# Hash-masked attention, capacity routing and two expert layers: late weight splits behind a gather, a fourth conversion buffer, projections in two units

## The chip, the cores and the metric

The kernel runs on one core of a Trainium2 chip. The metric is the device time of one execution in microseconds, taken as the median of several runs. Of the kernel before, three runs stand at 821.13, 822.87 and 824.08 us.

## The reference, cut to what matters

Three stages follow one another, and each needs the one before.

```python
# 1. attention, B=2, H=8, S=768, D=64: a query sees only keys of its own hash bucket
q_bits = (q @ proj > 0); k_bits = (k @ proj > 0)          # 6 bits each
scores = where(q_bucket == k_bucket, q @ k.T / sqrt(D), -1e9)
x = softmax(scores) @ v                                    # -> x of 1536 x 512
# 2. routing: 8 experts of 192 tokens each, then two layers per expert
assigned = greedy_by_logit(x @ w_gate, cap=192)
out[assigned == e] = relu(x[assigned == e] @ w1[e]) @ w2[e]   # 512 -> 1024 -> 512
# 3. a gated layer over all tokens
xn = out / rms(out) * rms_g
return (silu(xn @ w_gate2) * (xn @ w_val)) @ w_out         # 512 -> 1536 -> 512
```

The three weights of stage 3 arrive as 64-bit numbers; the kernel turns each of their blocks into 32-bit numbers itself.

## The kernel before, in words

**Attention.** There are eight pairs of heads (`p`), and each pair has twelve *units* (`u`, 96 in all): one unit is one head and one chunk of 128 queries. The loop at lines 601 to 621 writes, unit by unit, the exponential of the next unit, the transposes of this one (L361), the scores of the one after the next (L336 and L339), the product with the values (L380), and last whatever the table `fill` holds for that unit. So the scores of a pair's first unit are written in the unit that is the eleventh of the pair ahead of it (its unit 10, counting from 0).

`fill` carries three kinds of side work, each put at a unit by hand:

- *Preparing the next pair.* `SLOTS` gives six places, as units after the start of the pair that is running: four for `prep_t` (transposes, then on GpSimd a rounded part `nh` at L285 and a rest `nl` at L286), two for `prep_p` (six matmuls with the hash projections at L294, then a threshold on VectorE at L297). Right after the second `prep_t` of a tensor comes `prep_d`, six DMAs on SyncE's queue (L310 to L312). After the last `prep_p` comes `prep_s`, four DMAs (L320) that bring the hash bits into the second operand of the scores; one unit later `load_pair` issues three loads (L98). The first prepared pair uses `SLOTS1`, which stays as it is.
- *Converting weights of stage 3*, in 36 blocks (lines 528 to 532). Block n is loaded at unit n * 12 // 5 (`conv_load`, L242), converted five units later (`conv`: ScalarE L250, VectorE L253 and L254, then four GpSimd operations L255 to L258 on the tile `ha`), and stored to DRAM four units after that (`conv_store`, L263). The tile `ha` has three buffers.
- *Loading expert weights*: eight loads of 512 KB (`load_w`, L202 and L205), at units 20, 29, 38 and so on.

Within one unit of `fill` the order is: preparation, then conversion, then `load_w`. SyncE issues all of these DMAs in the order written.

**Routing and the experts.** After the last unit ScalarE rounds eight blocks of the first expert's weights (`split_hi`, L215); the rests (`split_lo`, L218: a subtraction on 128 x 1024 numbers) of blocks 0 to 3 are on VectorE (0 to 2 inside the routing rounds, 3 at line 925), and those of blocks 4 to 7 on GpSimd. Each `split_lo` also issues the load of the block eight further on. GpSimd fetches the tokens of the first two experts with three gathers (L890), a conditional block closes the routing, VectorE finishes the output indices (L921 to L923) and block 3's rest, ScalarE loads a table that waits for a small memset (L1053, L1104), and TensorE transposes the gathered rows (`gather_t`: L983; evacuated by ScalarE at L987 and VectorE at L988), between filler matmuls (L1101).

Then the experts run in *steps*, 16 per expert: eight of layer 1 (L1005, L1007) and eight of layer 2 (L1029, L1031). Layer 2's step 8 is the first that reads block 4, steps 10, 12 and 14 the first that read blocks 5, 6 and 7. Work is hung on steps by `at_step`; within one step the order is that of the calls:

```python
at_step(9, gather_t, 0, 2)
for n, i in enumerate(range(4, 8)):
    at_step(LATE[n], split_lo, i, True)      # rests of blocks 4..7 on GpSimd
...
at_step(t0 + WSTEP[n], split_w, 8 * (e + 1) + n, n in DVE_HI, n in POOL_LO)
...
at_step(t0 + 2 + 4 * kk, gather, j + 1, kk)  # steps 2, 6 and 10 of an even expert
```

`gather` has three row buffers, so the next gather waits until TensorE has transposed the first gather's rows. The next expert's first block (its rounding, L213 on VectorE, and its rest on GpSimd) is at step 4, the second at step 7.

**The gated layer** (L1194, L1222) follows with TensorE busy to the end.

Of the kernel before, what the change touches and what calls it, by code (L numbers as in the profile page):

```python
# [13 lines left out]
I32 = mybir.dt.int32  # L14
# [10 lines left out]
ACT_EVAC = 1  # L25
SLOTS1 = (0, 0, 4, 5, 5, 6)
CONV = 5
SLOTS = (-1, 0, 1, 3, 7, 7)
WSTEP = (4, 7, 9, 10, 10, 13, 15, 16)
POOL_LO = (0, 1, 4, 5, 7)  # L30
DVE_HI = (0, 4)
# [5 lines left out]
NORM = (10, 11, 12, 15)  # L37
N5 = (16, 16, 16, 16)
BB = 4
LATE = (0, 0, 1, 3)  # L40
MB = (5, 1, 2)
WB = (8, 0, 2, 0, 4, 4)
MINEXP = float(np.array([0x38100000], np.int32).view(np.float32)[0])
# [3 lines left out]
def lsh_attention__moe__swiglu_kernel(ctx, tc, q, k, v, proj, m_wg, m_w1, m_w2,  # L47
# [38 lines left out]
    cv = att.enter_context(tc.tile_pool(name="cv", bufs=2))  # L86
# [141 lines left out]
    for src, dst in ((f_wg, wg_d), (f_wv, wv_d), (f_wo, wo_d)):  # L228
        n = src.shape[0] * src.shape[1] // (128 * 512)
# [15 lines left out]
    def conv(n):  # L245
        w = CV[n]
        hi = w.bitcast(I32).rearrange("p (n t) -> p n t", t=2)[:, :, 1]
        lo = w.bitcast(U32).rearrange("p (n t) -> p n t", t=2)[:, :, 0]
        lr = cv.tile([128, 512], I32, name="lr")
        nc.scalar.activation(lr, lo, AF.Copy, scale=2.0 ** -29)  # L250
        ha = cv.tile([128, 512], I32, name="ha", bufs=3)
        sg = cv.tile([128, 512], I32, name="sg")
        nc.vector.tensor_scalar(ha, hi, 0x7fffffff, None, op0=OP.bitwise_and)  # L253
        nc.vector.tensor_scalar(sg, hi, -2 ** 31, 2 ** 30, op0=OP.bitwise_and, op1=OP.bitwise_or)  # L254
        nc.gpsimd.tensor_scalar(ha.bitcast(F32), ha.bitcast(F32), 3.0e38, MINEXP, op0=OP.min, op1=OP.max)  # L255
        nc.gpsimd.tensor_tensor(ha, ha, eight.to_broadcast([128, 512]), op=OP.mult)
        nc.gpsimd.tensor_tensor(ha, ha, lr, op=OP.add)
        nc.gpsimd.tensor_tensor(ha, ha, sg, op=OP.add)  # L258
        CV[n] = ha
# [251 lines left out]
    def at(u, f, *a):  # L511
        fill.setdefault(u, []).append((f, a))

    for p in range(1, NPAIR):
        u0 = (p - 1) * TPB * 2
        slots = iter(SLOTS if p > 1 else SLOTS1)
        for nm in "kq":
            for half in range(2):
                n = u0 + next(slots)
                at(n, prep_t, p, nm, half)  # L520
            at(n, prep_d, p, nm)
        for half in range(2):
            n = u0 + next(slots)
# [4 lines left out]
    for n in range(len(convs)):  # L528
        u = CONV + n * 12 // 5
        at(u - 5, conv_load, n)  # L530
        at(u, conv, n)
        at(u + 4, conv_store, n)
    for i in range(8):
        at(20 + i * 9, load_w, i)
    at(HP * TPB * 2 + 7, key_top)
# [456 lines left out]
    def at_step(t, f, *a):  # L992
        todo.setdefault(t, []).append((f, a))
# [118 lines left out]
    for n, i in enumerate(range(4, 8)):  # L1112
        at_step(LATE[n], split_lo, i, True)
    for e in range(E):
# [198 lines left out]
```

## Time and profile before

| what | value |
|---|---|
| median of three runs | 822.87 us (821.13 to 824.08) |
| the profiled execution | 824.88 us |
| span in its profile, first to last instruction | 822.8 us |
| mean granted clock of TensorE | 0.96 of full speed |
| TensorE busy | 768.2 us (93% of the span) |
| VectorE, ScalarE, GpSimd busy | 522.4, 396.1, 329.6 us |
| mean DMA rate | 140 GB/s |

The span is 2.1 us shorter than the profiled execution, which in turn is 2.0 us above the median. In the tables of the trace, "PE" is TensorE, "PEld" its weight loads, "DVE" VectorE, "ACT" ScalarE, "POOL" GpSimd and "SP" SyncE (a "q" behind it: the engine's queue). L12 is line 12 of the kernel. A bracket such as [2.41 <-DMA s_q<-sg] is idle time of that engine just before the instruction and what ended it; "issue" stands where the profile shows nothing that was waited for. A busy engine is not always at work: an instruction that is held by something else is shown as long.

### The profile page before, as it was taken

Reading aid. Unit: us, or ns where it says so; the run is one execution under the profiler, and the core shown is the slowest. Engines: PE = TensorE matmul, PEld = TensorE weight load, DVE = VectorE, ACT = ScalarE, POOL = GpSimd, SP = SyncE. Lnnn points to the kernel's source line nnn. Section 1 sums busy time; section 2 is a strip of 40 time slices with the busy share of each in tenths; the row PEclk is TensorE's granted clock in tenths of the full one; section 3 lists DMA queues with packets and bytes.
Section 4 is the critical chain, followed back from the end, with each engine's and each line's share of the span. In section 5 each row is a group of like instructions: output and inputs, shape, how many; then the busy total and the mean of one; then the engine's idle time right before and its main releaser. Section 6 shows DMA issues by size and latency. Waiting matters only on the chain.

```text
span 822.8 us, 14746 instructions
## 1 busy us (share of the span) xinstructions
PE 768.2 (93%) x5317; PEld 690.7 (84%) x5317; DVE 522.4 (63%) x1342; ACT 396.1 (48%) x863; POOL 329.6 (40%) x309
## 2 busy tenths in 40 slices
PE   7999989999989983489999999999999999999997
PEld 4788878887878863289999999999999999999996
DVE  7788977888768888648878778665422332233222
ACT  3677766676656762056776766653311211121111
POOL 3288876786767720736676652000100010001001
PEclk9999998999989995579999999999999999999999
DMA  3568896987869512247687844264200110001001
GB/s 78 172 205 225 260 252 198 271 255 250 231 205 267 186 39 77 76 170 232 226 269 235 272 148 142 69 223 145 77 1 1 38 39 1 1 1 39 1 0 39
DMA packets 89770, 115.58 MB, mean 140 GB/s; under 512 B 22124, under 2 KB 68188, under 8 KB 89692
## 3 DMA queue, kind: packets, MB, share of 16 engines
q1 hardware_dynamic: 87612, 108.28, 43.8%
q0 software_dynamic: 1920, 6.29, 2.2%
q8 instruction: 44, 0.72, 0.4%
q14 instruction: 34, 0.28, 0.1%
q10 hardware_dynamic: 160, 0.00, 0.0%
HBM read 77.62 MB, written 18.87 MB: 117 GB/s over the span
## 4 chain that ended last, share of the span: by engine, by line
PE 36%; issue 18%; POOL 1%; DVE 1%; ACT 1%; POOLq 0%; ACTq 0%; DVEq 0%
PE pg L1194 6%; PE pv L1194 6%; PE py L1029 6%; PE po L1222 6%; PE ph L1005 5%; PE py L1031 3%; PE ph L1007 3%; POOL out_dram L1230 1%; PE ph L983 1%; DVE wl L218 0%; PE px L1061 0%; POOL wl L218 0%; PE px L1084 0%; ACT bt L1015 0%; ACT sq L1047 0%
## 5 line engine op out<-in xcount | busy, mean ns | idle before, releaser
L1230 POOL DMA_INDIRECT out_dram<-ot,oi x12 | 11.7, 974 | 307.7 <-DVE ot L1228 306.2
L350 ACT ACTIVATE pr<-sc,rs 128x768 f32<-128x768 f32 x96 | 95.3, 993 | 61.9 <-DVE rs L343 35.4
L218 POOL TENSOR_TENSOR wl<-wr,wh 128x1024 fp32r<-128x1024 f32 x39 | 93.9, 2419 | 53.0 <-PE ph L1005 21.7
L341 DVE TENSOR_REDUCE rs<-sc 128x1 f32<-128x768 f32 x96 | 91.2, 950 | 24.6 <-PE sc L339 24.2
L1203 DVE TENSOR_TENSOR a<-sg,pg 128x384 f32<-128x384 f32 x48 | 26.6, 553 | 103.1 <-ACT sg L1201 103.1
L361 PE MATMUL m<-ident,pr 128*128 128x128 f32 x576 | 85.4, 284 | 5.7 <-ACT pr L350 2.6
L1005 PE MATMUL ph<-xg,wh 128*128 128x384 f32 x256 | 76.4, 368 | 8.8 <-issue 6.9
L380 PE MATMUL xo<-pt,ld_v 128*64 128x128 f32 x1128 | 83.9, 285 | 0.0
L361 PEld LDWEIGHTS m<-ident,pr 128*128 128x128 f32 x576 | 63.5, 142 | 20.6 <-issue 6.0
L380 PEld LDWEIGHTS xo<-pt,ld_v 128*64 128x64 f32 x1128 | 60.8, 138 | 19.2 <-issue 12.8
L1029 PE MATMUL py<-ht,wh 128*128 128x384 f32 x256 | 76.4, 363 | 0.0
L1201 ACT ACTIVATE sg<-pg 128x384 f32<-128x384 f32 x48 | 23.5, 490 | 106.0 <-PE pg L1194 105.9
L1207 ACT ACTIVATE ah<-a 128x384 fp32r<-128x384 f32 x48 | 25.2, 525 | 99.6 <-DVE a L1204 99.6
L1194 PE MATMUL pg<-xh,gl 128*128 128x384 f32 x192 | 64.6, 336 | 0.0
L1194 PE MATMUL pg<-xl,gh 128*128 128x384 f32 x192 | 64.6, 336 | 0.0
L1194 PE MATMUL pg<-xh,gh 128*128 128x384 f32 x192 | 64.6, 336 | 0.0
L1194 PE MATMUL pv<-xh,vl 128*128 128x384 f32 x192 | 64.4, 335 | 0.0
L1194 PE MATMUL pv<-xh,vh 128*128 128x384 f32 x192 | 64.4, 335 | 0.0
L1194 PE MATMUL pv<-xl,vh 128*128 128x384 f32 x192 | 64.4, 335 | 0.0
L1031 PE MATMUL py<-ht,wl 128*128 128x192 f32 x256 | 63.5, 253 | 0.0
L363 ACT ACTIVATE pt<-m 128x384 f32<-128x384 f32 x120 | 55.9, 488 | 6.8 <-PE m L361 6.8
L336 PE MATMUL sc<-s_k,s_q 128*128 128x384 f32 x192 | 58.3, 385 | 0.0
(252 smaller groups left out, 1961.3 us busy)
## 6 DMA issues: line engine op xcount, KB each, us to landing
wr<-in_moe_w_dram SPq DMA_DIRECT2D x64, 512.0 KB, 4.8
w<-in_moe_w_gate_dram SPq DMA_DIRECT2D x12, 512.0 KB, 4.9
w<-in_moe_w_val_dram SPq DMA_DIRECT2D x12, 512.0 KB, 5.5
w<-in_moe_w_out_dram SPq DMA_DIRECT2D x12, 512.0 KB, 5.7
s_k<-nh_k SPq DMA_DIRECT2D x28, 192.0 KB, 3.3
s_q<-nh_q SPq DMA_DIRECT2D x28, 192.0 KB, 3.6
ld_v<-in_v_dram SPq DMA_DIRECT2D x8, 384.0 KB, 6.2
wg_d<-ha SPq DMA_DIRECT2D x12, 256.0 KB, 4.7
```

The costliest lines, as they stand in the source:

```text
L218: (nc.gpsimd if pool else nc.vector).tensor_tensor(WL[i], WR.pop(i), WH[i], op=OP.subtract)
L336: nc.tensor.matmul(ps[:, n, :HALF], q1[:, h, qs], k1[:, h, n * HALF:(n + 1) * HALF], start=True, stop=False)
L341: nc.vector.tensor_reduce(rs[:, h, 0:1], ps[:, :, :HALF], axis=AX.XY, op=OP.min)
L350: nc.scalar.activation(pt, ps[:, :, :HALF], AF.Exp, scale=rs[:, h, 1:2], bias=rs[:, h, 2:3], accum_out=rs[:, h, 3:4])
L361: nc.tensor.transpose(t[:, i, :], pt[:, c * 128:(c + 1) * 128], ident)
L363: nc.scalar.activation(o[:, 3 * half:3 * half + 3, :], t, AF.Copy)
L380: nc.tensor.matmul(xo[64 * h:64 * h + 64], vt[:, h, chunk(p, c), :], a[h][:, c, :], start=(c == 0), stop=(c == TPB - 1))
L1005: hi = lambda: nc.tensor.matmul(ph[:, :2 * CAP], wh[:, d], xg[:, d].rearrange("p a b -> p (a b)"), start=(d == 0), stop=(d == KD - 1), ski ...
L1029: hi = lambda: nc.tensor.matmul(py[d][:, :2 * CAP], wh[:, ds], ht[:, f].rearrange("p a b -> p (a b)"), start=(f == 0), stop=(f == KF - 1), ...
L1031: lo = lambda: nc.tensor.matmul(py[d][:, :CAP], wl[:, ds], ht[:, f, 0], start=False, stop=False, skip_group_check=True)
L1194: nc.tensor.matmul(t[:, :TJ], a[:, d, :], b_[:, d, :], start=(n == 0), stop=(n == 3 * KD - 1))
L1222: nc.tensor.matmul(PO[j][t], a[:, ts], b_, start=(f == 0 and n == 0), stop=(f == KG - 1 and n == 2))
```

## The change

The rests of blocks 4 to 7 move from steps 0, 0, 1, 3 to steps 3, 3, 4, 5, that is behind the gather of step 2. The last two places of `SLOTS` move from unit 7 and 7 to units 5 and 6, and `prep_s` and `load_pair`, which follow the last of them, move from units 7 and 8 to units 6 and 7. The tile `ha` gets a fourth buffer, and each converted block is stored three units after its conversion instead of four.

```diff
-SLOTS = (-1, 0, 1, 3, 7, 7)
+SLOTS = (-1, 0, 1, 3, 5, 6)
...
-LATE = (0, 0, 1, 3)
+LATE = (3, 3, 4, 5)
...
-        ha = cv.tile([128, 512], I32, name="ha", bufs=3)
+        ha = cv.tile([128, 512], I32, name="ha", bufs=4)
...
-        at(u + 4, conv_store, n)
+        at(u + 3, conv_store, n)
```

## Rows read from the trace of the kernel before

**Rows 1.** The page, TensorE's granted clock in 40 slices of 20.6 us.

```profile
PEclk9999998999989995579999999999999999999999
```

**Rows 2.** Busy time by stretch: PE, PEld, DVE, ACT, POOL, then clock, DMA share, GB/s.

```profile
345.07:351.99 6.92, 0.00 (x0) 0.03 (x1) 4.45 (x7) 2.31 (x5) 5.51 (x3) 0.70 0.42 128
351.99:358.08 6.09, 6.09 (x23) 6.09 (x24) 1.83 (x5) 1.65 (x5) 0.00 (x0) 0.50 0.66 252
...
395.00:404.20 9.20, 9.20 (x64) 9.15 (x65) 8.51 (x23) 7.33 (x23) 5.79 (x4) 1.00 0.69 235
```

**Rows 3.** Timeline of TensorE, 341 to 352 us.

```profile
342.38 1.06 PE L983 MATMUL ph<-ident,xrow 128*128 128x128 f32 x4
...
343.66 0.97 PE L983 MATMUL ph<-ident,xrow 128*128 128x128 f32 x4
...
351.99 0.66 PE L1005 MATMUL ph<-xg,wh 128*128 128x384 f32 x1 [6.92 <-issue]
```

**Rows 4.** Timeline of ScalarE, 343 to 353 us.

```profile
350.20 0.85 ACT L987 ACTIVATE xg<-ph 128x512 fp32r<-128x512 f32 x2
```

**Rows 5.** Timeline of VectorE, 340 to 353 us.

```profile
340.35 6.65 DVE L921 TENSOR_SCALAR t<-rcs 128x12 f32<-128x12 f32 x1 [4.30 <-DVEq L911]
347.04 0.17 DVE L922 TENSOR_TENSOR t<-t,rcs 128x12 f32<-128x12 f32 x1
...
348.50 0.07 DVE L1053 MEMSET vv<- 128x10 f32 x1
```

**Rows 6.** Timeline of GpSimd, 336 to 362 us: start, duration, what.

```profile
340.02 6.95 POOL L218 TENSOR_TENSOR wl<-wr,wh 128x1024 fp32r<-128x1024 f32 x3
347.12 0.96 POOL L890 DMA_INDIRECT xrow<-x_d,gi  x1 [0.16 <-issue]
```

**Rows 7.** TensorE's waits for DMAs in the attention, and the stretch behind the first.

```profile
PE sc L339 <- DMA s_q<-sg: 4.8, 2, 2.4
...
122.50:129.40 6.90, 6.01 (x30) 5.00 (x32) 2.97 (x8) 1.57 (x3) 4.25 (x4) 0.51 0.95 344
```

**Rows 8.** Waits on the conversion tile, and of TensorE's transposes (total, times, longest).

```profile
  DVE ha L253: 9.6, 9
...
PE m L361 <- ACT pr L350: 2.6, 7, 0.9
```

**Rows 9.** Two shorter gaps of TensorE, from its timeline.

```profile
25.72 0.55 PE L278 MATMUL m<-ident,ld_k 128*128 128x128 f32 x3 [1.23 <-ACT pt L363]
...
499.61 0.44 PE L1005 MATMUL ph<-xg,wh 128*128 128x384 f32 x1 [0.97 <-DVE ht L1022]
```

**Rows 10.** VectorE's rounding of expert weights (ns min/median/max), and TensorE behind its longest.

```profile
L213 DVE CAST wh<-wr x14: 674/681/2121, 360.4 to 489.8; 128x1024 fp32r<-128x1024 f32 x14
...
381.61 0.44 PE L1005 MATMUL ph<-xg,wh 128*128 128x384 f32 x1 [0.89 <-DVE ht L1022]
```

**Rows 11.** The page, DMA issues: count, size, median us from issue to landing.

```profile
wr<-in_moe_w_dram SPq DMA_DIRECT2D x64, 512.0 KB, 4.8
```

**Rows 12.** GpSimd at the last rest of that pair, and TensorE's first work of the pair's unit 7.

```profile
107.84 1.01 POOL L286 TENSOR_TENSOR nl_q<-nr_q,nh_q 128x384 fp32r<-128x384 f32 x1
...
110.02 0.88 PE L361 MATMUL m<-ident,pr 128*128 128x128 f32 x6
```

**Rows 13.** Timeline of SyncE's queue, 84 to 140 us.

```profile
107.79 0.60 SPq L310 DMA_DIRECT2D s_q<-nh_q  x1
...
111.99 0.83 SPq L263 DMA_DIRECT2D wg_d<-ha  x1
...
113.90 0.99 SPq L202 DMA_DIRECT2D wr<-in_moe_w_dram  x1
114.94 0.50 SPq L263 DMA_DIRECT2D wg_d<-ha  x1
115.54 1.71 SPq L320 DMA_DIRECT2D s_k<-sg  x2
117.29 1.59 SPq L320 DMA_DIRECT2D s_q<-sg  x2
```

## The prediction, made before the changed kernel was run

> **What bounds the kernel now.** TensorE is busy for 768 of 822.8 us, so I looked for where it is not, or where it runs slowly. The first view is the clock line of the page [rows 1]: besides the routing (slices 15 to 17), only slices 6 and 11 show less than full clock. That gives three places, and everything else in the span is TensorE at work at its upper level of 2.4 GHz.
>
> The first place is the start of the experts. The windows show TensorE idle for 6.92 us, from 345.07 to 351.99, and then 6.09 us of layer 1 at a granted clock of 0.50, which is the lower level of 1.2 GHz [rows 2]. The chain of waits calls the idle time "issue", so I followed it backwards over the other engines. The first matmul needs the gathered rows, which TensorE had transposed by 344.63 [rows 3]. ScalarE copies them out only at 350.20 [rows 4], behind a table load that waits for VectorE's memset at 348.50. That memset is late because a VectorE instruction on 12 numbers per partition, L921, took 6.65 us, from 340.35 to 347.00; its neighbour L922, as small, took 0.17 [rows 5]. Over the same stretch GpSimd ran three rests back to back, from 340.02 to 346.97 [rows 6]. L921 ends 0.03 us after the third of them: I read it as held by GpSimd.
>
> The other two places are in the attention. Twice TensorE waits 2.4 us for the hash bits of the next pair (L339, waiting for the DMA out of `sg`), and behind the wait the clock stands at 0.51 for 6.9 us [rows 7]. This happens while pairs 3 and 6 are being prepared (units 24 to 35 and 60 to 71), the two cases in which a 512 KB expert load (units 29 and 65) falls between `prep_d` and `prep_s`. Below, a unit is counted from its pair's start. Some small gaps remain: TensorE's transposes wait for the exponential 7 times, 2.6 us in all, and VectorE waits 9 times, 9.6 us in all, for a buffer of `ha` [rows 8].
>
> **The rests behind the gather.** No instruction is added; four subtractions change places with one gather on GpSimd. After its three fetches GpSimd now meets the gather of step 2, which waits until TensorE has transposed the first rows, at 343.44 [rows 3]. So from 340.0 to about 343.6 GpSimd runs nothing, and L921 takes 0.17 us: it ends at 340.52, not 347.00. Today 3.20 us lie between its end and ScalarE's first copy (347.00 to 350.20), so that copy could start at 343.72. The second copy then has a later limit: the second group of transposes ends at 344.63 [rows 3]. Today the second of the two copies starts at about 350.63 (half of 0.85 after 350.20), and 1.36 us later TensorE starts at 351.99. Allowing 0.2 us for the handover from TensorE to ScalarE, TensorE starts at 344.63 + 0.2 + 1.36 = 346.2. **That is 5.8 us earlier.**
>
> Its gap shrinks from 6.92 to 1.1 us. Gaps of 1.23 and 0.97 us elsewhere [rows 9] left the clock at its upper level; the gaps of 2.4 us did not. The first is the near one, so I take the clock as staying up: layer 1 no longer runs 6.09 us at half speed, which saves half of that, **3.0 us** (bounds: nothing, or less than nothing if the clock falls later and longer; 3.0 at most).
>
> Against it stands what the four rests now lie beside. The gather ends about 344.55 and three rests of 6.95 us together end about 351.5. The next expert's first rounding on VectorE (step 4) normally takes 0.68 us and once took 2.12 when a rest of GpSimd was running, which cost TensorE 0.89 us [rows 10]. In the new order VectorE comes to it after step 3: at 346.2 + 4 steps of 1.15 (eight take 9.20 [rows 2]) + 0.9 for the sum of that step, 351.7. So it just misses the rests. I charge 0.2 us and keep 0 to 2.4 (one rest) for the range. The rests are in time: block 4 by 347.0 for step 8 at 355.4, block 7 (behind the next expert's first rest on GpSimd) by 357.4 for step 14 at 362.5. Each rest also releases a 512 KB load on SyncE's queue; the last is now issued about 357.4 instead of 351 and is read from step 16, near 365, and such a load lands in 4.8 us [rows 11]. Behind it on SyncE are only loads needed later. Sum: 5.8 + 3.0 - 0.2 = 8.6 us.
>
> The skill bears on this step. The Trainium skill, page "SBUF — State Buffer", section "Who interferes with whom", says that VectorE in certain forms (tensor_scalar among them) and GpSimd take turns at one pair of ports, and that the one that comes second is blocked until the first one's instruction is finished. The trace agrees that L921 was blocked, but it was blocked over three instructions, not one. By the rule as worded the hold would have ended with the first of the three, at about 342.3, and the rest of L921's time would have a cause that the move leaves in place: the move would give some 2 us in all. The row shows 6.65 us, so the sum goes by the row.
>
> **Projections in two units.** The same 12 matmuls and two thresholds per pair; the first half moves from unit 7 to 5, the second to 6, so TensorE's work is equal. The second half needs GpSimd's last rest `nl_q`, which ends at 108.85, while TensorE ends its unit 6 at about 110.0 [rows 12], so there is at least 1.1 us to spare, more with the first half now ahead of it. The four DMAs of `prep_s` can then be issued once SyncE reaches them, and there lies the catch. For pair 3 SyncE waits until 107.79 for GpSimd's half of `prep_d`, then issues without a pause: six DMAs, a store, a load, the 512 KB expert load, a store, and at 115.54 the first of `prep_s`, the last pair of which ends at 118.88 [rows 13]. The changed order puts ahead of `prep_s` the same DMAs: the store of unit 6 moves to unit 5, before the expert load instead of behind it, so moving `prep_s` to unit 6 passes nothing. Their bytes are the same too, and the DMA engines are still 0.95 busy right behind the wait [rows 7]. So `prep_s` starts at about 115.5 again and lands when it does now: **I take 0 for both long waits** (bounds: 1 us worse each, up to all of it). Where no wait stands today, nothing is won by an earlier landing. `load_pair` (three DMAs) now precedes one conversion load; both have units of slack.
>
> **Four buffers, stored sooner.** Nothing is added but space. VectorE's nine waits on `ha` should go. VectorE is not the bound, so the 9.6 us are not the gain; what is late next is the exponential, which TensorE awaits for 2.6 us in all [rows 8]. The part of it just ahead of the two long waits would only lengthen those, so I take **0.8 us**, between 0 and 1.4. A store now waits sooner for GpSimd on SyncE; what follows it is a load of the next block or a `prep_d` that waits longer for GpSimd anyway.
>
> **Sum:** 8.6 + 0.8 = 9.4 us. The profiled execution of 824.88 us (span 822.8) would come to 815.5; against the median of 822.87, that is 813.5 us. The forecast's own range is 811 to 816.
>
> **The rivals.** *The long waits go too.* If SyncE or the DMA engines get `prep_s` through even 1 or 2 us sooner, the waits shrink below what lowers the clock. Each costs 2.4 us plus half of the slow 6.9 us less the 0.9 in which TensorE still waited (to 123.4), 5.4 us; both together 10.8: 802.7 us, one alone 808.1. For it: today's thresholds end only just before SyncE gets to `prep_s`. Against it: SyncE has no pause ahead of it.
>
> *The clock falls all the same* in the gap of 1.1 us: the 5.8 us stay, the 3.0 are lost and up to 2 more: today's slow stretch is longer than the part that layer 1 pays, since a mean clock of 0.70 over the gap of 6.92 us means 4.1 of it at half, 10.2 with the 6.09 [rows 2]. That gives about 817.5. For it: the filler before is thinner than the dense work before the two short gaps.
>
> *L921 is long for another reason* (or the rule as worded holds): then 0 to 2 us remain, and the kernel is near 821.5, about the same. Against it: the coincidence of the two ends, to 0.03 us.
>
> *Slower:* the second projection, two matmul groups ahead of where it stood, reaches TensorE before GpSimd has written `nl_q`. The place is unit 6 of six pairs. The margin is 1.1 us, and past a wait of some 2 us each pair would pay 5.4 us as above. It decides from GpSimd being some 3 us later than now: three or more pairs at 5.4 us then outweigh the 9.4, six of them make the kernel 846 us. Against it: GpSimd's order up to `nl_q` is unchanged.
>
> **How the numbers follow.** Chances: forecast 0.63, long waits go 0.17, clock falls 0.10, no hold 0.05, slower 0.05. The predicted time is the first, 813.5 us. The range takes in the second and third with their spread: 801.5 to 818.5, leaving out 0.1. About 0.3% (2.5 us) is what a measurement of this kernel can tell from no change. Faster by more: 0.63 + 0.17 + 0.10 = 0.90; within: 0.05; slower: 0.05.
>
> **What would show it.** Right: L921 at 0.17 us, TensorE's gap before the first L1005 near 1 us, layer 1 of the first expert in about 9.3 us, no wait of L253 for a store, and L339 still waiting near 2.4 us for pairs 3 and 6 with the clock down behind it. Wrong: no slow stretch left in the attention, a slow stretch behind 346 us, or a wait of the projection matmuls for GpSimd.

## The result, and the profile of the changed kernel

The changed kernel takes 813.91 us (median of five runs, 811.05 to 815.83) where the kernel before takes 822.87 (821.13 to 826.30, five runs): a ratio of 0.9876, 95% interval 0.9851 to 0.9902. The forecast was 813.5 us. Its profiled execution took 814.53 us, with a span of 812.7.

The span is 10.1 us shorter. To see where, I cut both traces at the same four events: the first unit's transposes in the attention, those of the last unit, the filler matmul with which TensorE starts behind the routing (the *join*), and the first matmul of the third expert.

| stretch | before | after | change | predicted |
|---|---|---|---|---|
| start to the first unit | 22.64 | 22.11 | -0.5 | 0 |
| attention, units 0 to 95 | 277.23 | 273.76 | -3.5 | -0.8 |
| end of attention to the join | 40.43 | 40.27 | -0.2 | 0 |
| join to the third expert | 54.62 | 48.41 | -6.2 | -8.6 |
| third expert to the end | 427.9 | 428.2 | +0.3 | 0 |

So the total is right, but two of its parts are not: the experts gave 2.4 us less than forecast, the attention 2.7 us more. The sections below are about these two differences. Each column is one execution, and the attention varies more than this from one execution to the next: the kernel before's attention code took 277.23, 278.29 and 281.72 us in three profiles (before, e1, e5), the changed kernel's 273.76 and 272.72 in two (change, e6).

First the page's clock line of the changed kernel, beside [rows 1]:

```profile
PEclk8999999999999995699999999999999999999999
```

The two dips inside the attention (slices 6 and 11) are no longer seen at this grain, and slice 17 has filled. Next the windows, with the columns of [rows 2]: layer 1 of the first expert, the whole of it, the second expert, then the stretch behind TensorE's first long wait in the attention and one behind its longest, and last the whole attention.

```profile
341.37:350.89 9.52, 9.52 (x64) 9.27 (x65) 5.90 (x15) 4.97 (x15) 8.89 (x5) 1.00 0.67 188
341.37:360.50 19.13, 19.13 (x133) 18.88 (x133) 12.64 (x23) 10.63 (x23) 15.37 (x8) 1.00 0.68 205
360.50:384.55 24.05, 21.95 (x144) 21.38 (x143) 17.59 (x39) 14.84 (x35) 17.60 (x8) 0.93 0.73 228
124.80:128.20 3.40, 3.40 (x21) 3.07 (x20) 1.70 (x5) 1.57 (x3) 0.89 (x1) 0.50 1.05 402
232.10:238.00 5.90, 5.90 (x53) 5.06 (x53) 3.62 (x12) 3.19 (x8) 2.41 (x4) 1.00 0.93 352
22.11:295.87 273.76, 260.51 (x2334) 220.12 (x2332) 222.91 (x659) 190.82 (x421) 198.43 (x206) 0.99 0.79 225
```

The same three windows of the kernel before (first expert, second expert, attention):

```profile
351.99:373.67 21.68, 21.68 (x132) 21.68 (x133) 11.26 (x23) 10.86 (x23) 7.77 (x4) 0.86 0.49 165
373.67:394.92 21.25, 20.36 (x143) 19.80 (x142) 17.58 (x39) 14.76 (x35) 16.43 (x8) 1.00 0.74 236
22.64:299.87 277.23, 264.77 (x2335) 222.95 (x2333) 226.59 (x659) 188.97 (x421) 198.60 (x206) 0.98 0.77 222
```

The gap is 0.66 us instead of 6.92 and the clock stays at its upper level behind it; the first expert is 2.55 us shorter. But the second expert is **2.8 us longer**, at a mean clock of 0.93. The timelines of VectorE, GpSimd and TensorE in the changed kernel say why (start, duration, what):

```profile
336.20 0.17 DVE L921 TENSOR_SCALAR t<-rcs 128x12 f32<-128x12 f32 x1 [4.02 <-DVEq L911]
...
346.93 1.24 DVE L213 CAST wh<-wr 128x1024 fp32r<-128x1024 f32 x1
...
355.38 3.38 DVE L218 TENSOR_TENSOR wl<-wr,wh 128x1024 fp32r<-128x1024 f32 x2 [0.26 <-ACT wh L215]
...
359.43 1.23 DVE L218 TENSOR_TENSOR wl<-wr,wh 128x1024 fp32r<-128x1024 f32 x1
...
365.99 3.35 DVE L213 CAST wh<-wr 128x1024 fp32r<-128x1024 f32 x1
```

```profile
339.56 0.94 POOL L890 DMA_INDIRECT xrow<-x_d,gi  x1 [3.45 <-PE ph L983]
340.53 7.08 POOL L218 TENSOR_TENSOR wl<-wr,wh 128x1024 fp32r<-128x1024 f32 x3
...
354.12 2.42 POOL L218 TENSOR_TENSOR wl<-wr,wh 128x1024 fp32r<-128x1024 f32 x1
359.50 3.42 POOL L218 TENSOR_TENSOR wl<-wr,wh 128x1024 fp32r<-128x1024 f32 x1 [2.96 <-issue]
...
364.04 4.73 POOL L218 TENSOR_TENSOR wl<-wr,wh 128x1024 fp32r<-128x1024 f32 x2
```

```profile
341.37 0.41 PE L1005 MATMUL ph<-xg,wh 128*128 128x384 f32 x1 [0.66 <-issue]
...
369.65 0.44 PE L1005 MATMUL ph<-xg,wh 128*128 128x384 f32 x1 [2.10 <-DVE ht L1022]
```

L921, 6.65 us long before [rows 5], takes 0.17 while GpSimd waits 3.45 us for the transposes. In the second expert two of GpSimd's rests run from 364.04 to 368.77. VectorE's rounding for the third expert starts at 365.99, in the middle of them, and ends at 369.34, 0.57 us after the second; 0.68 is what it takes undisturbed [rows 10]. TensorE waits 2.10 us for VectorE behind it instead of 0.89 [rows 10], and from 370.56 the clock is at half for 3.41 us: 1.2 us of wait and 1.7 of clock make the 2.8.

The two rests are not those that were moved. These fill GpSimd in the first expert (15.37 us busy instead of 7.77) and are done at 352.99; the two belong to the second expert's own weights. They stood beside this rounding before as well: the 2.12 us of [rows 10] are the same rounding. But they now end 8.27 us behind the start of the second expert, where they ended 7.07 behind it. GpSimd was idle for 2.96 us ahead of 359.50, so this is no plain queue on GpSimd; the two engines hold each other in turn. The kernel before has these lines in the place of those at 355.38 and 359.50:

```profile
368.56 2.36 DVE L218 TENSOR_TENSOR wl<-wr,wh 128x1024 fp32r<-128x1024 f32 x2 [0.26 <-ACT wh L215]
...
371.66 2.39 POOL L218 TENSOR_TENSOR wl<-wr,wh 128x1024 fp32r<-128x1024 f32 x1 [4.55 <-PE py L1031]
```

The late rests push GpSimd's rest of 354.12 beside VectorE's two, which take 3.38 us instead of 2.36. The rounding behind those two, and with it the rest at 359.50 that reads its result, come 1.0 us later by the second expert's start. There VectorE's rest of 359.43 is first by 0.07 us, and GpSimd's takes 3.42 us instead of 2.39. The gather behind it is 0.8 us shorter, so 1.2 us of delay are left for the two rests.

### The profile page after: what moved, and what is told of

Same layout as the page of the kernel before. It is cut to its first block, busy times and chain, and to the rows that moved or that the text cites. A ratio compares the mean times of both kernels' runs of the same rounds, so it can differ in the third digit from the quotient of the medians.

```text
span 812.7 us, 14759 instructions
## 1 busy us (share of the span) xinstructions
PE 761.3 (94%) x5317; PEld 685.2 (84%) x5317; DVE 513.7 (63%) x1342; ACT 398.0 (49%) x863; POOL 328.6 (40%) x309
## 3 DMA queue, kind: packets, MB, share of 16 engines
HBM read 77.62 MB, written 18.87 MB: 119 GB/s over the span
## 4 chain that ended last, share of the span: by engine, by line
PE 37%; issue 18%; POOL 1%; DVE 1%; ACT 1%; POOLq 0%; ACTq 0%; DVEq 0%
PE pg L1194 6%; PE pv L1194 6%; PE py L1029 6%; PE po L1222 6%; PE ph L1005 6%; PE py L1031 3%; PE ph L1007 3%; POOL out_dram L1230 1%; PE ph L983 1%; PE py L1101 0%; DVE wl L218 0%; PE px L1061 0%; PE px L1084 0%; ACT bt L1015 0%; DVE yn L1091 0%
## 5 line engine op out<-in xcount | busy, mean ns | idle before, releaser
L361 PE MATMUL m<-ident,pr 128*128 128x128 f32 x576 | 83.4, 281 | 3.1 <-ACT pt L363 2.5
L1005 PE MATMUL ph<-xg,wh 128*128 128x384 f32 x256 | 75.3, 363 | 3.8 <-DVE ht L1022 3.1
L361 PEld LDWEIGHTS m<-ident,pr 128*128 128x128 f32 x576 | 63.8, 141 | 15.1 <-issue 7.4
L215 ACT ACTIVATE wh<-wr 128x1024 fp32r<-128x1024 f32 x50 | 51.2, 1054 | 14.2 <-PE py L1029 11.4
L339 PE MATMUL sc<-s_k,s_q 82*128 82x384 f32 x192 | 49.9, 341 | 8.7 <-DMA s_q<-sg 8.7
```

The costliest lines, as they stand in the source:

```text
L215: nc.scalar.activation(WH[i], WR[i], AF.Copy)
L339: nc.tensor.matmul(ps[:, n, :HALF], q2[:64 + NS, h, qs], k2[:64 + NS, h, n * HALF:(n + 1) * HALF], start=False, stop=True)
L361: nc.tensor.transpose(t[:, i, :], pt[:, c * 128:(c + 1) * 128], ident)
L1005: hi = lambda: nc.tensor.matmul(ph[:, :2 * CAP], wh[:, d], xg[:, d].rearrange("p a b -> p (a b)"), start=(d == 0), stop=(d == KD - 1), ski ...
```

## The experiments

Each kernel was timed in five rounds beside the kernel before, and all ratios are to that kernel. Where a split by stretches is given, it is that of one profiled execution, cut as above.

| kernel | ratio | 95% interval | median, us | attention, us | join to third expert, us |
|---|---|---|---|---|---|
| change | 0.9876 | 0.9851 to 0.9902 | 813.91 | 273.76 | 48.41 |
| e1 rests alone | 0.9932 | 0.9907 to 0.9957 | 819.29 | 278.29 | 48.29 |
| e2 projections alone | 0.9942 | 0.9918 to 0.9966 | 818.86 | 271.49 | 54.75 |
| e3 buffer and store alone | 0.9973 | 0.9949 to 0.9997 | 822.91 | 275.37 | 54.53 |
| e4 change, two loads later | 0.9807 | 0.9772 to 0.9842 | 808.32 | 266.24 | 46.78 |
| e5 L921 moved, rests not | 0.9950 | 0.9927 to 0.9972 | 820.82 | 281.72 | 45.57 |
| e6 change, block 4 on VectorE | 0.9878 | 0.9851 to 0.9905 | 814.12 | 272.72 | 45.91 |
| e7 change, stores as before | 0.9814 | 0.9781 to 0.9848 | 808.40 | 266.59 | 48.40 |
| e8 e4, e6 and e7 together | 0.9735 | 0.9708 to 0.9762 | 802.29 | 262.18 | 46.07 |
| e9 e8, a rounding on ScalarE | 0.9746 | 0.9718 to 0.9774 | 801.01 | 263.05 | 45.03 |
| e10 before, two loads later | 0.9933 | 0.9914 to 0.9952 | 817.33 | 270.45 | 54.01 |
| e11 e8 with three buffers | 0.9836 | 0.9806 to 0.9867 | 808.30 | 267.77 | 46.07 |

The profiled execution need not be a typical one: e4's took 805.38 us and e6's 811.65, 2.9 and 2.5 below their medians, e5's 822.34, 1.5 above. The medians of the kernel before were 824.58 (beside e1 to e4), 825.28 (e5 to e8) and 822.49 us (e9 to e11).

**e1, the rests alone.** The kernel before with one edit.

```diff
-LATE = (0, 0, 1, 3)
+LATE = (3, 3, 4, 5)
```

> The kernel before with the late rests alone. Theory: L921 falls from 6.65 to 0.17 us, TensorE starts layer 1 some 6.4 us sooner after the join, layer 1 of the first expert takes 9.5 us instead of 12.1, and the second expert gives 2 to 3 us back behind the rounding L213, which GpSimd's later rests hold: about 6.2 us in all, 816.7 us. The attention is as before, with two waits of 2.4 us and the clock down behind both. Rival: the rests are the whole change, and the attention's part was chance: 814 us.

Measured 0.9932. The first expert starts 5.22 us behind the join (5.23 in the changed kernel). The windows of e1 with the columns of [rows 2]: first expert, second expert.

```profile
346.23:365.26 19.03, 19.03 (x132) 18.87 (x133) 12.52 (x23) 10.63 (x23) 15.27 (x8) 1.00 0.64 210
365.26:389.30 24.04, 21.95 (x144) 21.38 (x143) 17.70 (x39) 14.87 (x35) 17.61 (x8) 0.93 0.69 227
```

The two experts are those of the changed kernel to 0.1 us, so both the gain and the loss of 2.8 us belong to this edit alone. Its attention, with no edit in it, took 278.29 us where the kernel before shows 277.23, and the clock fell there for 3.41 us behind each wait, not for 6.83. A difference of 1 us between two attentions is therefore nothing to explain.

**e2, the projections alone.**

```diff
-SLOTS = (-1, 0, 1, 3, 7, 7)
+SLOTS = (-1, 0, 1, 3, 5, 6)
```

> The kernel before with the projections in units 5 and 6 alone. Theory: the bits are not issued sooner for pairs 3 and 6, their waits stay at 2.4 to 3 us; the earlier issue right behind other DMAs is what brings the new waits of 1.3 to 1.5 us of pairs 2 and 4; the small gaps ahead of the transposes shrink. Sum near nothing: 821 to 824 us. Rival: the split of the projections is what speeds the attention by 3.5 us: 819 us.

Measured 0.9942, 5.7 us off the attention: my theory fell, and the rival holds. TensorE waits for the bits 3 times, 2.6 us in all and 1.1 at most. The timelines of e2, of SyncE's queue and TensorE around pair 3:

```profile
114.77 1.05 SPq L202 DMA_DIRECT2D wr<-in_moe_w_dram  x1
115.91 1.71 SPq L320 DMA_DIRECT2D s_k<-sg  x2
117.67 1.60 SPq L320 DMA_DIRECT2D s_q<-sg  x2
119.31 0.47 SPq L263 DMA_DIRECT2D wg_d<-ha  x1
...
122.94 0.59 PE L339 MATMUL sc<-s_k,s_q 82*128 82x384 f32 x2 [1.05 <-DMA s_q<-sg]
```

In [rows 13] the store of L263 stands between the expert load and `prep_s`; here it stands behind. I count from the moment when TensorE comes to the scores, its start less its wait. Before the change (L339 starts at 123.39 after a wait of 2.41) that is 120.98, with the last issue of `prep_s` ending 2.10 us earlier, at 118.88 [rows 13], and the bits there 4.51 us after it. In e2 it is 121.89, the issue ends 2.62 us earlier, at 119.27, and the bits are there after 3.67. So they are issued 0.5 us sooner by TensorE's measure, and land 0.8 us quicker: the wait is 1.05 instead of 2.41, and no half clock is left in the attention.

**e3, the buffer and the store alone.**

```diff
-        ha = cv.tile([128, 512], I32, name="ha", bufs=3)
+        ha = cv.tile([128, 512], I32, name="ha", bufs=4)
...
-        at(u + 4, conv_store, n)
+        at(u + 3, conv_store, n)
```

> The kernel before with the fourth buffer and the earlier stores alone. Theory: the nine waits of L253 for a store go, part of the 2.6 us of gaps ahead of the transposes goes, the two long waits stay with the clock down behind them: 821.5 to 823 us. Rival: the earlier stores free the queue and shorten the long waits: 816 to 818 us.

Measured 0.9973, about 2 us off. TensorE's transposes no longer wait for the exponential in the loop (2.6 us before [rows 8]), but its waits for the bits grow from 4.8 us [rows 7] to 7.5, the longest 3.7 (the list of waits).

The ratios of the three edits alone multiply to 0.9932 x 0.9942 x 0.9973 = 0.985; together they measure 0.9876. That is inside the spread of three such intervals, so the ratios alone show no interaction; what the earlier stores cost beside the moved projections is measured by e7.

**e7, the change with the stores where they were** (four buffers kept).

```diff
-        at(u + 3, conv_store, n)
+        at(u + 4, conv_store, n)
```

> The changed kernel with the stores of converted blocks back at four units after the conversion, the four buffers kept. The store of unit 6 then stands behind the hash bits on the queue and not ahead of them. Theory: that one store of 256 KB is what the projections' move gains on the queue and what the earlier store took back; the waits of pairs 3 and 6 fall from about 2.9 to 1 us and no slow stretch follows: 2.5 to 5 us less than the changed kernel, ratio 0.982 to 0.985 to the kernel before. Rival: the waits go with chance and not with the store: as the changed kernel, ratio 0.988.

Measured 0.9814, an interval that does not touch the change's. The timelines of SyncE's queue and TensorE around pair 3, first of the changed kernel, then of e7:

```profile
114.22 0.65 SPq L263 DMA_DIRECT2D wg_d<-ha  x1
114.92 1.21 SPq L202 DMA_DIRECT2D wr<-in_moe_w_dram  x1
116.22 1.71 SPq L320 DMA_DIRECT2D s_k<-sg  x2
117.97 1.59 SPq L320 DMA_DIRECT2D s_q<-sg  x2
...
123.87 0.59 PE L339 MATMUL sc<-s_k,s_q 82*128 82x384 f32 x2 [2.87 <-DMA s_q<-sg]
```

```profile
112.95 0.61 SPq L202 DMA_DIRECT2D wr<-in_moe_w_dram  x1
113.66 1.71 SPq L320 DMA_DIRECT2D s_k<-sg  x2
115.41 1.59 SPq L320 DMA_DIRECT2D s_q<-sg  x2
117.05 0.46 SPq L263 DMA_DIRECT2D wg_d<-ha  x1
...
120.19 0.59 PE L339 MATMUL sc<-s_k,s_q 82*128 82x384 f32 x2 [0.49 <-DMA s_q<-sg]
```

The waits for the bits (total, times, longest), of the changed kernel and of e7:

```profile
PE sc L339 <- DMA s_q<-sg: 8.7, 4, 3.0
```

```profile
PE sc L339 <- DMA s_q<-sg: 3.1, 3, 1.3
```

The two kernels differ only in where the stores stand: all 36 move by one unit, and the fences show the one next to pair 3's bits. With it behind, `prep_s` ends 2.70 us before TensorE comes (117.00, 119.70) instead of 1.44 (119.56, 121.00), and lands 3.19 us after its issue instead of 4.31. The attention is 7.2 us shorter. The earlier store gives back some 5 us (0.9876 - 0.9814 of 825 us) of what the projections' move had won.

**e4, two expert loads later**, in the changed kernel: the 512 KB loads at units 29 and 65 go to 31 and 67, behind `prep_s`.

```diff
-    for i in range(8):
-        at(20 + i * 9, load_w, i)
+    for i, u in enumerate((20, 31, 38, 47, 56, 67, 74, 83)):
+        at(u, load_w, i)
```

> The changed kernel with two expert loads moved from units 29 and 65, where they stand just ahead of the hash bits, to units 31 and 67, just behind them. Theory: what makes pairs 3 and 6 wait is the 512 KB load ahead of the bits on the queue; their waits fall from 2.9 and 3.0 us to about the 1.4 of pairs 2 and 4, and the slow stretch behind the first goes: 3 to 5 us less than the changed kernel, 809 to 811 us. Rival: the bits wait for the thresholds or for GpSimd, and not for the load: waits and time as in the changed kernel, 814 us.

Measured 0.9807, 7.5 us off the attention. SyncE's queue around pair 3 and, in the second fence, the window of the second expert:

```profile
112.80 0.64 SPq L263 DMA_DIRECT2D wg_d<-ha  x1
113.53 1.71 SPq L320 DMA_DIRECT2D s_k<-sg  x2
115.29 1.59 SPq L320 DMA_DIRECT2D s_q<-sg  x2
118.99 0.42 SPq L202 DMA_DIRECT2D wr<-in_moe_w_dram  x1
```

```profile
352.94:375.39 22.45, 20.36 (x143) 19.79 (x142) 17.49 (x39) 14.77 (x35) 17.63 (x8) 1.00 0.77 245
```

Pair 3 waits no more, pair 6 for 1.9 us, the only wait for the bits that is left. The expert load ahead of the bits is thus the other half of the cause. In the second expert, whose code is the change's, the rounding is held for 3.33 us and TensorE waits 2.09 us, as there, but the clock stays up and the expert is 1.6 us shorter than there. So of the 2.8 us lost in the second expert only the 1.2 of wait recur in every profile with these rests; the part of the clock is in three (change, e1, e7) and not in e4's.

**e10, the same later loads in the kernel before.**

> The kernel before with the two expert loads moved behind the hash bits alone, nothing of the change. Theory: the order on the queue is what made both long waits, and the units of the projections do not matter for it: both waits fall below 1 us, the clock stays up in the attention, 9 to 11 us less than before, ratio 0.987 to 0.989. Rival: without the earlier projections the bits are still late: waits over 1.5 us, ratio over 0.993.

Measured 0.9933. No wait of L339 for the bits is left, as my theory has it, but the price was the rival's: the attention gains 6.8 us in the profile and the ratio comes to 5.5 us. Other gaps came up: the transposes wait 4.1 us for the exponential instead of 2.6 [rows 8], and those of the pair being prepared (L278) 2.0 us for its loads.

```profile
PE m L361 <- ACT pr L350: 4.1, 7, 1.0
```

**e5, another way past the hold.** The kernel before, rests where they were on GpSimd; instead what VectorE does ahead of the memset is taken away: L921 to L923 go to step 24, block 3's rest to step 0.

```diff
-    nc.vector.tensor_scalar(t3, rcs[:, 1], float(TPB), float(S - TPB), op0=OP.is_ge, op1=OP.mult)
-    ...
-    split_lo(3, False)
+    def scatter_rows():
+        nc.vector.tensor_scalar(t3, rcs[:, 1], float(TPB), float(S - TPB), op0=OP.is_ge, op1=OP.mult)
+        ...
+    at_step(0, split_lo, 3, False)
+    at_step(24, scatter_rows)
```

> The kernel before, its rests on GpSimd left where they are, but VectorE's path to the first matmul cleared of what takes two inputs or a fast form from on-chip memory: L921 to L923 move to step 24 and block 3's rest to step 0, so that the memset comes first. Theory: only such forms are held by GpSimd's rests; TensorE starts layer 1 about 5.2 us after the join instead of 11.6, layer 1 runs at full clock, and the second expert gives nothing back beyond its 0.9 us gap: about 9 us less than before, ratio 0.989. Rival: whatever VectorE runs there is held until GpSimd is done: no gain, ratio 1.00.

In the trace it is as expected: the join to the third expert takes 45.57 us, 9.05 less than before. The timelines of GpSimd, VectorE and TensorE of e5 behind the join at 344.47 (its lines stand two further down: L1055, L990 and L1007 are L1053, L988 and L1005 elsewhere):

```profile
344.18 6.99 POOL L218 TENSOR_TENSOR wl<-wr,wh 128x1024 fp32r<-128x1024 f32 x3
...
344.56 0.07 DVE L1055 MEMSET vv<- 128x10 f32 x1 [4.34 <-DVEq L911]
348.16 1.02 DVE L990 TENSOR_TENSOR xg<-ph,xg 128x512 fp32r<-128x512 f32 x2 [3.54 <-ACT xg L989]
349.98 2.28 DVE L218 TENSOR_TENSOR wl<-wr,wh 128x1024 fp32r<-128x1024 f32 x1
...
349.29 0.41 PE L1007 MATMUL ph<-xg,wh 128*128 128x384 f32 x1 [0.76 <-POOL wl L218]
```

TensorE starts the first expert 4.82 us after the join. GpSimd runs its three rests from 344.18 to 351.17, and VectorE's memset (0.07 us) and L990's two subtractions (1.02 together), which read one operand from PSUM, run beside them. Block 3's rest, which starts at 349.98 while they still run, takes 2.28 us; in the kernel before it took 1.22. So it was L921 and what hangs on it that held the start, not GpSimd's load as such. But the time shows only half, 0.9950. In that profile the unchanged attention took 281.72 us, 4.5 more than before, and the third expert to the end 2.4 more. In the attention the time lies in TensorE's waits: 7.2 us for the bits instead of 4.8 [rows 7], and 5.8 of the transposes for the exponential instead of 2.6 [rows 8]. What made them longer in code that was not edited I can't say, nor what made the end longer, and the miss stands.

**e6, block 4's rest on VectorE** in the changed kernel, behind the memset, to take one of the rests off GpSimd.

```diff
+    split_lo(4, False)
...
-    for n, i in enumerate(range(4, 8)):
-        at_step(LATE[n], split_lo, i, True)
+    for n, i in enumerate(range(5, 8)):
+        at_step(LATE[n + 1], split_lo, i, True)
```

> The changed kernel with the rest of block 4 on VectorE, behind the memset, where VectorE is idle for 2.3 us, instead of on GpSimd. Theory: GpSimd's queue in the first expert is one rest of 2.4 us shorter, the rounding L213 in the second expert is held for less than the 3.35 us of the changed kernel, TensorE's gap of 2.1 us there falls to 0.9 or less and the slow stretch behind it goes: 2 to 3 us less than the changed kernel, ratio 0.985 to the kernel before. Rival: the gap comes from the order of the work on VectorE and not from GpSimd's backlog: as the changed kernel, ratio 0.988.

The window of the second expert, and in the second fence VectorE's rounding in it:

```profile
359.70:381.69 21.99, 20.37 (x143) 19.80 (x142) 18.76 (x39) 14.48 (x35) 17.14 (x8) 1.00 0.78 245
```

```profile
365.20 2.86 DVE L213 CAST wh<-wr 128x1024 fp32r<-128x1024 f32 x1
```

The second expert is 2.1 us shorter, at full clock, though the rounding is still held and TensorE still waits 1.62 us. Of the 2.1 only some 0.5 are wait; the rest is the clock, which stays up in e4 without this edit. The time, 0.9878, does not differ from the change's: the gain isn't shown in time, and the interval of 0.5% (4.5 us) is too wide to deny it.

**e8, together:** the change with e4's loads, e7's stores and e6's rest.

> The changed kernel with three edits: stores at four units, the two expert loads behind the hash bits (units 31 and 67), the rest of block 4 on VectorE. Theory: no wait for the hash bits over 0.5 us in any pair, TensorE's clock at its upper level from the first pair to the routing and from the join to the end; about 9 us less than the changed kernel, ratio 0.977. Rival: the gains overlap, and it is no better than the changed kernel with the loads moved alone, ratio 0.981.

802.29 us, ratio 0.9735. The window of the attention:

```profile
22.62:284.80 262.18, 257.47 (x2335) 218.97 (x2333) 222.28 (x659) 190.63 (x421) 198.53 (x206) 1.00 0.81 235
```

No wait for the bits is left, the clock is up, and the attention is 15 us shorter than before. The second expert takes 21.99 us, as in e6.

**e9, the held rounding on ScalarE**, on top of e8.

```diff
-                at_step(t0 + WSTEP[n], split_w, 8 * (e + 1) + n, n in DVE_HI, n in POOL_LO)
+                at_step(t0 + WSTEP[n], split_w, 8 * (e + 1) + n, n in DVE_HI and (e, n) != (1, 0), n in POOL_LO)
```

> The kernel of all three edits (802.3 us) with the third expert's first rounding on ScalarE instead of VectorE, so that GpSimd's rests hold nothing there. Theory: TensorE's gap of 1.63 us in the second expert falls below 0.5, nothing else changes: 1 to 2 us less, ratio 0.971 to the kernel before. Rival: ScalarE's 1.05 us at that place delays the copies of the sums as much as the hold did: no gain, ratio 0.9735.

The window of the second expert:

```profile
350.64:371.09 20.45, 20.37 (x143) 19.80 (x142) 16.06 (x38) 15.15 (x36) 17.05 (x8) 1.00 0.86 267
```

Next to no gap is left in it: 20.45 us, 20.37 of them TensorE's work. So the gap that e8 still had came from the held rounding. The time, 801.01 us or 0.9746, can't be told from e8's. These two are the best versions run, some 12 us below the change.

**e11, e8 with three buffers of** `ha`.

> The kernel of all three edits with three buffers of the converted weights instead of four. Theory: VectorE waits for stores again, 9 times or so and 6 to 10 us in all, TensorE's gaps ahead of the transposes come back: 2 to 4 us more, ratio 0.976 to 0.978. Rival: the buffer does nothing once the projections are spread: ratio 0.9735.

Measured 0.9836, 1% slower than e8 and more than I expected; the attention is 5.6 us longer. VectorE's waits on the tile `ha` (total, times) are back, and with them five waits of TensorE's transposes, 2.3 us in all:

```profile
  DVE ha L253: 8.8, 11
```

The list of TensorE's waits has this row of L361 in the six kernels with three buffers (before, e1, e2, e5, e10, e11: 2.3 to 5.8 us) and in none with four.

## Why the prediction was right, and where its steps failed

**The start of layer 1: right.** From L921's start to the first L1005 it is 5.17 us (336.20 to 341.37) instead of 11.64, so 6.5 us less; forecast 5.8. I had allowed 0.2 us for the handover and a gap of 1.1; the gap is 0.66.

**Layer 1 at full clock: right.** 3.0 less 0.2 were forecast, and the first expert is 2.55 us shorter; its layer 1 takes 9.52 us, about 9.3 were forecast.

**The held rounding: the term that was mis-sized, and put in the wrong place.** "I charge 0.2 us and keep 0 to 2.4" looked at the rounding in the first expert only. There it was caught after all, because TensorE started 0.7 us sooner by the join than I had reckoned, and took 1.24 us, at no cost that shows: the first expert takes 19.13 us, and 18.87 to 19.17 in e6, e8 and e9, where that rounding takes 0.68. The cost of 2.8 us lies one expert later, in the very rounding whose 2.12 us I had quoted [rows 10]: the moved rests shift the work of GpSimd and VectorE against each other in the first expert, and the two rests over the second expert's rounding end 1.2 us later. Runs on both sides carry the hold: e1 has it with the rests' edit alone, in e5, where the rests stay, it is 2.13 us as before, e6 lightens it, and in e9, where that rounding is off VectorE, the gap is gone. Of the 2.8 us, the 1.2 of wait follow from it; the 1.6 of clock came with it in three profiles out of four (not in e4). The bound for one rest, 2.4, was a little low for the sum: the hold lasted into a second rest, and I had put no clock into the term.

**L921 held by GpSimd: right; the page's rule, weighed.** The trace and e5 agree with what the move assumes: with GpSimd idle L921 takes 0.17 us, and with L921 out of the way the start is early though GpSimd is busy. The Trainium skill, page "SBUF — State Buffer", section "Who interferes with whom", lets the blocked engine go on when the other's instruction is finished; the trace does not agree, neither for L921 before (6.65 us over three rests, [rows 5, 6]) nor for the rounding after (3.35 us into the end of the second of two). The measurement decides: the hold went to the end of the run of rests.

**The projections: the step that failed.** "Moving `prep_s` to unit 6 passes nothing" holds for the three edits together, and there the two long waits are still there as forecast, 2.87 and 3.0 us. But it hides that the projections' edit alone does pass a store (e2, 5.7 us of attention), and that the store's edit takes the place back (e7). I had written down that the store goes ahead and had not priced it as a loss of the change's own; e7 says some 5 us.

**The attention's 3.5 us for a forecast of 0.8.** The gaps ahead of the transposes are gone (-2.6 [rows 8]). The waits for the bits grew from 4.8 [rows 7] to 8.7 us (+3.9), two of them new, at pairs 2 and 4, of 1.3 to 1.5 us. The half clock behind the waits shrank from 13.66 us in all (twice 6.83), in 2.0 of which TensorE still waited, to 3.41: (13.66 - 2.0) / 2 - 3.41 / 2 = 4.1 us less. Together -2.8 of the -3.5. So the largest part is the clock, and that part I did not forecast. It may be no part of the change: the untouched attention had 6.8 us at half in e1 and 10.2 in e5, not 13.7, and the changed one 6.8 in e6. The other terms move as much between profiles: the transposes' waits for the exponential were 5.1 us in e1 and 5.8 in e5 with nothing edited there, and e6 waits for the bits at pairs 3, 6 and 7, not at 2 and 4. So the profiles at hand put the attention's change anywhere between 3.5 and 9 us.

**Four buffers, "0.8 us, between 0 and 1.4": too small, as far as the runs tell.** With the earlier store they gave about 2 us alone (e3), but its interval, 0.2 to 4.2 us, still holds 0.8. Where the bits are in time the fourth buffer is worth 5.6 us of attention (e11). I had taken 1.8 us off for gaps that would merely lengthen the waits.

So that 813.5 was met to 0.4 us is in part luck: the start of the experts came as forecast, but the second expert lost 2.8 us and the attention gave about as much more. Two of the signs named in advance fell on the wrong side: a slow stretch behind 346 us did come, at 370.56 in the second expert, and behind pair 6's wait of 3.0 us the clock did not fall. What happens at the experts' start is shown by e1, e5 and e9. The attention's sum is only partly understood.

**Left open:** why pairs 2 and 4 wait in the changed kernel's profile and not in e6's; why a wait of some 2 to 3 us lowers the clock at one time and not at another; what made the waits of e5's profile longer where nothing was edited; and whether e6 and e9 save time at all.

## What to carry to other kernels

When work is moved on one of two engines that hold each other, follow both on, past the place where it lands and past idle time between: the cost came a whole expert later. When a small transfer is awaited, list what stands ahead of it on its queue after *all* edits, and price each large neighbour by itself, since two edits that each help can undo one another there. And when a total is met, cut both traces at the same events before believing the terms, and see how far a stretch that nobody edited differs between two profiles.

## What the runs showed of the hardware that was not expected

- VectorE was held for as long as GpSimd's rests followed one another: 6.65 us over three, 3.35 us into the end of two. A memset (0.07 us) and a subtraction with one operand in PSUM (1.02 us for two) ran beside them (e5).
- Of two rests that met, the later one was held, on either engine: in the changed kernel VectorE's started 0.07 us ahead and took 1.23 us, GpSimd's 3.42; in the kernel before GpSimd's was 0.95 us ahead and took 2.39, VectorE's 2.53.
- Storing the 256 KB blocks one unit later, which for pair 3 puts one store behind four 54 KB transfers on SyncE's queue instead of ahead of them, was worth 0.6% of the kernel (e7 against the change).
- TensorE's clock behind a wait was not settled by the wait's length: 2.41 us before was followed by 6.83 us at half, 2.87 in the changed kernel by 3.41, and 3.0 at pair 6 by none; in the second expert 2.10 (change) was followed by 3.41, 2.09 (e4) by none.
- The attention of the same code took 277.23, 278.29 and 281.72 us in three profiles (before, e1, e5).
